# Attention scan and two expert layers in one program: all transfers on SyncE's and ScalarE's queues, a chunk's period of 25 steps, and ScalarE alone reading the stages' sums

## The chip, the cores and the metric

The kernel runs on one core of a Trainium2 chip. The metric is the device time of one execution in microseconds (us), and the figure for a kernel is the median over its runs. The core has five instruction streams that run side by side and meet only at semaphores: TensorE (PE in the profile, with its weight loads as PEld), VectorE (DVE), ScalarE (ACT), GpSimd (POOL) and SyncE (SP). A transfer is issued by an instruction in one of these streams and then carried out by the core's 16 DMA engines. Each stream works strictly in order, so an instruction that waits holds up all that stands behind it in its stream.

## What is computed

Three layers follow each other on 3072 tokens (4 sequences of 768) of 384 features. First comes a linear attention with a complex decay, whose state is 48 x 48 for each of 8 heads:

```python
for t in range(S):
    ar, ai = (a_re_n[:, :, t, :, None], a_im_n[:, :, t, :, None])
    new_re = ar * S_re - ai * S_im
    new_im = ar * S_im + ai * S_re
    kv = np.einsum('bhd,bhe->bhde', k[:, :, t], v[:, :, t])
    S_re, S_im = (new_re + kv, new_im)
    y[:, :, t] = np.einsum('bhd,bhde->bhe', q[:, :, t], S_re)
```

Then four experts, `out += p[:, e] * (relu(x @ w1[e]) @ w2[e])`, each with 1024 hidden features, and at last `max(0.01 * h, h) @ w_out` with `h = x @ w_in` and 2048 hidden features. The weights of the last layer arrive as 64-bit numbers.

## The kernel before

**The dense layers are the frame.** The tokens are worked in 6 groups of 512. A hidden block of 128 features is a *unit*: units 0 to 31 are the four experts (the first stage of a group), units 32 to 47 the last layer (the second stage). `order` (lines 357 to 365) lists all units of all groups: the first stages of groups 0, 1 and 2, then the second stage of group 0, and from there a first stage and the second stage of two groups earlier in turn, with the last two second stages at the end. The first 8 units of group 0 are run in two halves of 256 tokens. To keep accuracy, each operand is split into a high and a low part, so a unit costs 18 matmuls of 512 columns: 9 in `gemm_in` (L421) into `ph`, from which VectorE and ScalarE make `hp` and its parts `hh` and `hl` (L426 to L439), and 9 in `gemm_out` (L450 to L452), which add to the three sums `acc`. `gemm_in` runs two units ahead of `gemm_out`.

**Weights.** The experts' weights are loaded once (`raw`, L380), split by ScalarE and GpSimd (L396, L397), stored split in `ws_scratch` (L400), and loaded from there whenever the unit comes up again (L388), five units ahead, into 7 buffers. The last layer's weights are decoded from 64-bit numbers in the background (`decode`), loaded at L324 and stored at L351.

**Ends of stages.** At the end of a first stage the three sums become the input of the second: ScalarE copies each to `x2h` (L591) and VectorE subtracts it from the sum to give `x2l` (L592). At the end of a second stage ScalarE copies each sum to `o`, which has two buffers, and issues its transfer to the output (L601, L602). The next stage's first product into a sum waits until the sum has been read.

**The attention runs in between.** A chunk is 128 tokens; there are 24, four to a group. `elementwise(c)` makes the decayed features `ft` from the inputs `aaqk` on VectorE, ScalarE and GpSimd, and its last step sends `ft` in six transfers into `hd` (L247), which has the heads' features on the partitions. `products(c)` transposes `ft` (`pt`, L261), multiplies the features in `hd` to scores `sc` (L274), and goes on to `y`. Both are generators; `background()` calls one step at a time. Chunks 0 to 3 follow the written-out order `PLAN`. From chunk 4 on, a period of 23 calls and one empty one holds the 8 steps of `products(c)` at the calls in `PSTEPS` and the steps of `elementwise(c + 1)` at the others. `pace` spreads the calls evenly over the units, up to 3 behind each half of a unit, so that a group's four chunks are ready when its first stage begins. The program fixes the order within each stream; nothing is reordered at run time.

**Which queue issues what, before.** SyncE: the inputs, the raw and split weights, `hd` of chunks 0 to 3. GpSimd: `hd` from chunk 4 on and two of chunk 1, the stores of the split weights, and all of the decoder's transfers. ScalarE: the output.

## Time and profile before

| what | value |
|---|---|
| median of 3 runs | 1519.18 us (1519.04 to 1524.72) |
| the profiled execution | 1522.4 us, of which 1520.7 us are the span from its first to its last instruction |
| TensorE busy | 1414.4 us, 93% of the span |
| VectorE busy | 875.1 us, 58% |
| ScalarE busy | 557.1 us, 37% |
| GpSimd busy | 350.2 us, 23% |
| read and written in HBM | 262.72 MB and 42.52 MB |
| granted TensorE clock, mean over the span | 0.971 of full speed |

The busy shares are means over stages with different limits: the first 85 us are filled by the start of the attention, up to 640 us the attention of the next groups runs beside first stages, up to 1130 us beside first and second stages in turn, and behind that dense units stand alone. Sums of waits say who waited for whom, but a wait costs time only where the waiting engine sets the end. TensorE's clock has two levels, 1.2 and 2.4 GHz; the profile gives the granted clock of a stretch as a mean share of the higher one.

### The profile page before, as it was taken

Reading aid. Unit: us, or ns where it says so; the run is one execution under the profiler, and the core shown is the slowest. Engines: PE = TensorE matmul, PEld = TensorE weight load, DVE = VectorE, ACT = ScalarE, POOL = GpSimd, SP = SyncE. Lnnn points to the kernel's source line nnn. Section 1 sums busy time; section 2 is a strip of 40 time slices with the busy share of each in tenths; the row PEclk is TensorE's granted clock in tenths of the full one; section 3 lists DMA queues with packets and bytes.
Section 4 is the critical chain, followed back from the end, with each engine's and each line's share of the span. In section 5 each row is a group of like instructions: output and inputs, shape, how many; then the busy total and the mean of one; then the engine's idle time right before and its main releaser. Section 6 shows DMA issues by size and latency. Waiting matters only on the chain.

```text
span 1520.7 us, 18523 instructions
## 1 busy us (share of the span) xinstructions
PE 1414.4 (93%) x6972; PEld 1183.8 (78%) x6972; DVE 875.1 (58%) x1521; ACT 557.1 (37%) x939; POOL 350.2 (23%) x451
## 2 busy tenths in 40 slices
PE   1898998998998999899999999999999999999996
PEld 0797877786877887687888887888887888887875
DVE  8848777668888787875554554554533333332331
ACT  4535554434334333354233344233332111332232
POOL 5134677334333333321111111111100000000000
PEclk9789999999999999999999999999999999999998
DMA  6398778787778979768568568567556665555551
GB/s 245 50 290 283 247 250 261 220 271 214 241 271 249 285 262 289 208 217 244 180 209 238 170 197 244 180 203 208 157 183 205 210 196 196 195 187 180 187 195 44
DMA packets 75235, 325.49 MB, mean 214 GB/s; under 512 B 10464, under 2 KB 16448, under 8 KB 75136
## 3 DMA queue, kind: packets, MB, share of 16 engines
q1 hardware_dynamic: 56960, 253.10, 53.2%
q0 software_dynamic: 15584, 66.40, 14.8%
q10 hardware_dynamic: 2592, 4.72, 0.9%
q8 instruction: 56, 0.92, 0.3%
q14 instruction: 43, 0.35, 0.1%
HBM read 262.72 MB, written 42.52 MB: 201 GB/s over the span
## 4 chain that ended last, share of the span: by engine, by line
PE 62%; DVE 16%; DMA 6%; ACT 5%; issue 5%; POOL 4%; SPq 0%; ACTq 0%; DVEq 0%; POOLq 0%
PE ph L421 27%; PE acc L450 9%; PE acc L452 9%; PE acc L451 9%; DMA hd<-ft 4%; DVE hl L439 3%; PE sc L274 2%; PE py L297 2%; PE py L299 2%; DMA out_dram<-o 2%; ACT hh L438 2%; DVE hp L426 1%; DVE ft L238 1%; PE pm L285 1%; POOL hd L247 1%
## 5 line engine op out<-in xcount | busy, mean ns | idle before, releaser
L421 PE MATMUL ph<-xh,wt 128*128 128x512 f32 (+1 forms) x1200 | 400.7, 390 | 1.9 <-ACT wt L396 0.9
L450 PE MATMUL acc<-hh,wt 128*128 128x512 f32 (+1 forms) x888 | 357.2, 402 | 23.1 <-DVE x2l L592 11.0
L452 PE MATMUL acc<-hl,wt 128*128 128x512 f32 (+1 forms) x888 | 346.6, 390 | 3.3 <-DVE hl L439 3.0
L451 PE MATMUL acc<-hh,wt 128*128 128x512 f32 (+1 forms) x888 | 345.3, 389 | 0.0
L438 ACT CAST hh<-hp 128x512 fp32r<-128x512 f32 (+1 forms) x296 | 180.3, 609 | 416.7 <-DVE hp L426 345.0
L439 DVE TENSOR_TENSOR hl<-hp,hh 128x512 fp32r<-128x512 f32 (+1 forms) x296 | 218.3, 737 | 195.4 <-ACT hh L438 194.5
L421 PEld LDWEIGHTS ph<-xh,wt 128*128 128x128 f32 x1200 | 228.4, 193 | 45.8 <-ACT wt L396 1.1
L421 PE MATMUL ph<-xl,wt 128*128 128x512 f32 (+1 forms) x600 | 231.9, 386 | 0.0
L426 DVE SCALAR_TENSOR_TENSOR hp<-ph,pb 128x512 f32<-128x512 f32 (+1 forms) x200 | 133.1, 665 | 171.0 <-PE ph L421 170.5
L450 PEld LDWEIGHTS acc<-hh,wt 128*128 128x128 f32 x888 | 170.2, 192 | 57.7 <-ACT o L601 12.1
L452 PEld LDWEIGHTS acc<-hl,wt 128*128 128x128 f32 x888 | 169.6, 191 | 41.9 <-DVE hl L439 7.5
L421 PE MATMUL ph<-x2h,wt 128*128 128x512 f32 x576 | 199.0, 400 | 0.0
L451 PEld LDWEIGHTS acc<-hh,wt 128*128 128x128 f32 x888 | 170.6, 192 | 30.3
L429 DVE SCALAR_TENSOR_TENSOR hp<-hp 128x512 f32<-128x512 f32 x96 | 68.6, 715 | 180.9 <-ACT hp L428 180.9
L421 PEld LDWEIGHTS ph<-xl,wt 128*128 128x128 f32 x600 | 115.9, 193 | 21.0 <-DVE xl L316 0.3
L421 PEld LDWEIGHTS ph<-x2h,wt 128*128 128x128 f32 x576 | 109.4, 190 | 25.3
L428 ACT COPY hp<-ph 128x512 f32<-128x512 f32 x96 | 56.2, 585 | 176.3 <-PE ph L421 175.5
L421 PE MATMUL ph<-x2l,wt 128*128 128x512 f32 x288 | 115.0, 399 | 0.0
L247 POOL DMA_DIRECT2D hd<-ft x122 | 64.9, 540 | 151.0 <-DVE ft L238 112.5
L274 PE MATMUL sc<-hd 96*128 96x128 f32 x384 | 57.8, 300 | 24.7 <-DMA hd<-ft 20.9
L274 PEld LDWEIGHTS sc<-hd 96*128 96x128 f32 x384 | 55.3, 212 | 30.8 <-issue 13.2
L397 POOL TENSOR_TENSOR wt<-raw,wt 128x384 fp32r<-128x384 f32 x64 | 68.9, 1094 | 41.8 <-ACT wt L396 41.4
(98 smaller groups left out, 1525.2 us busy)
## 6 DMA issues: line engine op xcount, KB each, us to landing
wt<-ws_scratch SPq DMA_DIRECT2D x264, 768.0 KB, 4.6
ws_scratch<-wt POOLq DMA_DIRECT2D x32, 768.0 KB, 7.2
aaqk<-in_attn_dram SPq DMA_DIRECT2D x22, 768.0 KB, 8.6
hd<-ft POOLq DMA_DIRECT2D x122, 128.5 KB, 9.4
raw<-in_w_dram SPq DMA_DIRECT2D x32, 384.0 KB, 6.7
r<-in_w_dram POOLq DMA_DIRECT2D x32, 384.0 KB, 5.1
ws_scratch<-dw POOLq DMA_DIRECT2D x32, 384.0 KB, 5.6
pb<-pn_scratch SPq DMA_DIRECT2D x24, 256.0 KB, 5.0
```

The source lines that it names most:

```text
L247: (G if c >= CPG or c in HDG and i == ri else SP).dma_start(hd[row : row + DG], ft[:, ri, i])
L274: PE.matmul(sc[:, j], hd[:, h, P : 2 * P], hd[:, h, :P], start=True, stop=True)
L397: G.tensor_tensor(wt[:, 1], raw, wt[:, 0].bitcast(F32), ALU.subtract)
L421: PE.matmul(ph[:, : t1 - t0], wt[:, wi, cols], x[kc][:, t0:t1], start=n == 0, stop=n == 3 * NG - 1)
L426: V.scalar_tensor_tensor(hp, ph, 0.0, pbs[g, u // 8][:, t0:t1], ALU.max, ALU.mult)
L428: A.copy(hp, ph)
L429: V.scalar_tensor_tensor(hp, hp, 0.01, hp, ALU.mult, ALU.max)
L438: A.copy(hh, hp)
L439: V.tensor_tensor(hl, hp, hh.bitcast(F32), ALU.subtract)
L450: PE.matmul(out, wt[:, 0, cols], hh, start=first, stop=False)
L451: PE.matmul(out, wt[:, 1, cols], hh, start=False, stop=False)
L452: PE.matmul(out, wt[:, 0, cols], hl, start=False, stop=last)
```

## The change

All transfers that GpSimd issued go to SyncE (two of chunk 1 to ScalarE). The transfers into `hd` move from the end of `elementwise(c)` into a step of their own, `by_head`, at call 1 of the next period for chunks from 4 on. The store of a unit's split weights moves from the end of its splitting to the unit's own place in the order, in front of `gemm_out`. In the decoder the next load comes one call later, and a store is issued one block later. A period has 16 elementwise steps and 9 steps of products, 25 calls and an empty one: the phase's scan, its reduction to one turn and its limits are three steps, and the two halves of `ft` are two. `vt` has its buffers beside those of `aaqk`. At the end of a stage ScalarE copies the three sums, one behind the other, to `o`, which has three buffers; at a first stage's end `x2h` is a copy of `o` and `x2l` is made from both by GpSimd.

```diff
...
 DEC = 33.0
-PSTEPS = (3, 7, 8, 11, 13, 15, 18, 22)
-NSTEPS = 23
+PSTEPS = (1, 3, 5, 8, 10, 13, 16, 18, 21)
+ESTEPS = 16
+NSTEPS = ESTEPS + len(PSTEPS)
 WAIT = 4
...
                 t = pool.tile([P, 4, NG, P], F32, name="aaqk", bufs=2)
-                vt = p_in.tile([P, DM], F32, name="vt", bufs=4)
+                vt = pool.tile([P, DM], F32, name="vt", bufs=2 if c in (1, 3) else 3)
                 inputs[c] = (t, vt)
...
                 V.tensor_tensor_scan(th[:, i], ones, r[:, i], first, ALU.mult, ALU.add)
+            if c >= CPG:
+                yield
             V.tensor_scalar(g, th, 1.0 / TWO_PI, MAGIC, ALU.mult, ALU.add)
...
             T.tensor_tensor(th, th, g, ALU.subtract)
+            if c >= CPG:
+                yield
             V.tensor_scalar(th, th, -PI, PI, ALU.max, ALU.min)
...
                 )
-            yield
+                if i or c >= CPG:
+                    yield
+            feats[c] = (ft, vt)
+            if c < CPG:
+                by_head(c)
+        def by_head(c):
+            ft, vt = feats[c]
+            pool = p_el2 if c in (1, 3) else p_el
             hd = pool.tile([2 * D, H, 2 * P + 1], F32, name="hd")
...
                     row = ri * D + i * DG
-                    (G if c >= CPG or c in HDG and i == ri else SP).dma_start(hd[row : row + DG], ft[:, ri, i])
+                    (A if c in HDG and i == ri else SP).dma_start(hd[row : row + DG], ft[:, ri, i])
             feats[c] = (ft, hd, vt)
...
         def products(c):
+            if c >= CPG:
+                by_head(c)
+                yield
             ft, hd, vt = feats.pop(c)
...
                 raw64[i] = pools["dec"].tile([P, DM, 2], I32, name="r64", bufs=3)
-                G.dma_start(
+                SP.dma_start(
                     raw64[i].rearrange("p a b -> p (a b)"),
...
                 )
+        stored = []
...
             G.tensor_tensor(wt[:, 1], wo, wt[:, 0].bitcast(F32), ALU.subtract)
+            yield
             load_raw64(i + 3)
-            yield
-            G.dma_start(ws[NU1 + u][:, half], wt.bitcast(F32))
+            if stored:
+                SP.dma_start(*stored.pop())
+            stored.append((ws[NU1 + u][:, half], wt.bitcast(F32)))
...
                 del raws[s]
-                G.dma_start(ws[order[s][1]], wts[s].bitcast(F32))
...
                     yield from decode(i)
+                yield
+                SP.dma_start(*stored.pop())
...
             for g in range(1, NGRP):
-                pace.append((begins[g] - MARGIN, first + 14 + (NSTEPS + 1) * CPG * g))
+                pace.append((begins[g] - MARGIN, first + ESTEPS + (NSTEPS + 1) * CPG * g))
             pace.append((1e9, pace[-1][1] + 1))
...
                 return u in (NU1, NU1 + 1) and order[s - 1 - (u - NU1)][:2] == (g, NU1 - 1)
+            def evacuate(acc):
+                out = [pools["x2"].tile([P, TG], F32, name="o", bufs=NG) for _ in acc]
+                for o, a in zip(out, acc):
+                    A.copy(o, a)
+                return out
...
                 split_h(s + 2, hp)
+                if fresh[s]:
+                    SP.dma_start(ws[u], wts[s].bitcast(F32))
                 gemm_out(s, acc)
...
                 if u == NU1 - 1:
+                    evacuated = evacuate(acc)
                     x2[g] = ([], [])
-                    for dc in range(NG):
+                    for dc, o in enumerate(evacuated):
                         xh = pools["x2"].tile([P, TG], F32R, name=f"x2h{dc}", bufs=LAG + 1)
                         xl = pools["x2"].tile([P, TG], F32R, name=f"x2l{dc}", bufs=LAG + 1)
-                        A.copy(xh, acc[dc])
-                        V.tensor_tensor(xl, acc[dc], xh.bitcast(F32), ALU.subtract)
+                        A.copy(xh, o)
+                        G.tensor_tensor(xl, o, xh.bitcast(F32), ALU.subtract)
                         x2[g][0].append(xh)
...
                 elif u == NU - 1:
-                    for dc in range(NG):
-                        o = pools["x2"].tile([P, TG], F32, name="o", bufs=2)
-                        A.copy(o, acc[dc])
+                    for dc, o in enumerate(evacuate(acc)):
                         A.dma_start(outT[dc * P : (dc + 1) * P, g * TG : (g + 1) * TG], o)
...
```

## Rows read from the trace of the kernel before

**Rows 1.** Busy us by engine (instructions), granted clock, DMA share, GB/s; a late stretch

```profile
1300.00:1340.00 40.00, 40.00 (x175) 32.68 (x175) 15.34 (x23) 13.53 (x23) 0.00 (x0) 1.00 0.57 193
```

**Rows 2.** TensorE's waits from 100 to 440 us: total us, times, longest

```profile
PE sc L274 <- DMA hd<-ft: 19.2, 5, 5.8
```

**Rows 3.** TensorE's waits in the whole span, same columns

```profile
PE acc L450 <- DVE x2l L592: 11.0, 2, 6.4
PE acc L450 <- ACT o L601: 10.0, 5, 3.2
```

**Rows 4.** The view of rows 1 for stretches around waits of TensorE

```profile
139.00:154.00 15.00, 12.41 (x64) 10.81 (x63) 11.04 (x16) 6.18 (x11) 8.37 (x10) 0.77 0.95 329
...
288.00:303.00 15.00, 11.25 (x62) 9.72 (x61) 8.03 (x17) 5.01 (x7) 1.86 (x2) 0.89 0.70 222
374.00:390.00 16.00, 10.16 (x44) 8.70 (x44) 12.38 (x23) 7.90 (x14) 6.12 (x8) 0.79 0.88 293
468.00:485.00 17.00, 12.39 (x57) 10.41 (x56) 14.12 (x27) 6.68 (x13) 3.61 (x6) 0.90 0.79 285
633.00:650.00 17.00, 10.58 (x40) 8.33 (x39) 10.92 (x19) 8.64 (x16) 6.51 (x11) 0.80 0.99 225
...
1371.00:1384.00 13.00, 9.84 (x31) 7.54 (x30) 2.77 (x4) 3.00 (x5) 0.00 (x0) 0.74 0.50 168
```

**Rows 5.** Line 790, the program's end: count, ns min/median/max, first and last start

```profile
L790 POOLq DRAIN  x3: 50/107/9215, 1510.6 to 1520.4; - x3
L790 SPq DRAIN  x3: 7/7/7, 1512.9 to 1520.1; - x3
```

**Rows 6.** Timeline, a second stage's end: start, us, instruction, idle before and releaser

```profile
1369.57 0.59 ACT L601 COPY o<-acc 128x512 f32<-128x512 f32 x1 [0.46 <-ACT o L601]
...
1374.59 0.59 ACT L601 COPY o<-acc 128x512 f32<-128x512 f32 x1 [4.43 <-DMA out_dram<-o]
...
1375.22 0.80 PE L450 MATMUL acc<-hh,wt 128*128 128x512 f32 x1 [3.16 <-ACT o L601]
```

**Rows 7.** Timeline, a first stage's end (629 to 643 us)

```profile
630.91 1.82 DVE L238 TENSOR_TENSOR ft<-cs,aaqk 128x768 f32<-128x768 f32 x2
...
638.64 1.55 ACT L591 CAST x2h<-acc 128x512 fp32r<-128x512 f32 x3
...
639.38 1.88 DVE L592 TENSOR_TENSOR x2l<-acc,x2h 128x512 fp32r<-128x512 f32 x3
...
640.12 0.80 PE L450 MATMUL acc<-hh,wt 128*128 128x512 f32 x1 [6.42 <-DVE x2l L592]
```

**Rows 8.** Timeline, chunk 8 from its features to its scores (270 to 293 us)

```profile
271.97 1.82 DVE L238 TENSOR_TENSOR ft<-cs,aaqk 128x768 f32<-128x768 f32 x2
...
274.38 3.31 POOL L247 DMA_DIRECT2D hd<-ft  x6 [1.89 <-DVE hl L439]
...
292.51 0.77 PE L274 MATMUL sc<-hd 96*128 96x128 f32 x2 [3.75 <-DMA hd<-ft]
```

**Rows 9.** Issues of hd (columns: rows 11) from 0:100, 360:426, 1030:1110 us

```profile
hd<-ft SPq DMA_DIRECT2D x22, 128.5 KB, 5.6
...
hd<-ft POOLq DMA_DIRECT2D x12, 128.5 KB, 12.0
...
hd<-ft POOLq DMA_DIRECT2D x12, 128.5 KB, 6.7
```

**Rows 10.** Line 247, columns as in rows 5

```profile
L247 POOL DMA_DIRECT2D hd<-ft x122: 530/532/714, 42.0 to 1097.3; - x122
...
L247 SPq DMA_DIRECT2D hd<-ft x22: 547/601/688, 37.0 to 81.0; - x22
```

**Rows 11.** DMA issues of the whole span: count, KB each, median us to landing

```profile
wt<-ws_scratch SPq DMA_DIRECT2D x264, 768.0 KB, 4.6
ws_scratch<-wt POOLq DMA_DIRECT2D x32, 768.0 KB, 7.2
```

**Rows 12.** SyncE's waits in the whole span: total us, times, longest

```profile
SPq L147 <- DVE ft L238: 30.4, 10, 6.0
```


## The prediction

> **What bounds the kernel now.** The span is bounded by TensorE (PE), so the views were read in this order: what TensorE waited for, what its clock was after each wait, and then the place of each wait. In an undisturbed late stretch TensorE issues 175 matmuls of 512 columns in 40 us [rows 1], which is 0.229 us each, or 4.11 us for a unit of 18. Nothing in the change makes that stream shorter, so a gain can come only from time in which TensorE stands still or runs slowly. The list of waits has three entries that the change touches: the scores (`sc`) wait for the transfer into `hd`, 19.2 us in 5 waits between 100 and 440 us [rows 2]; the first product of a new stage waits for `x2l` (11.0 us in 2) and for `o` (10.0 us in 5) [rows 3]. Behind such a wait the granted clock falls to the lower level, 1.2 GHz, for some us: the stretch from 139 us has a mean granted share of 0.77, so 15 x 0.23 = 3.45 us of full speed are missing [rows 4]. Four stretches around the waits for `hd` are like this (0.77 three times, 0.79 once over 16 us) and one of 15 us has 0.89: 3 x 3.45 + 3.36 + 1.65 = 15.4 us. The two waits for `x2l` cost 17 x 0.10 + 17 x 0.20 = 5.1 us in this way, and of those for `o` only the one at 1375 us, 13 x 0.26 = 3.4 us [rows 4]. The last view is the end of the program: GpSimd's (POOL's) drain takes 9.2 us from 1510.6, while SyncE (SP) is at its own drain, 0.007 us long, at 1512.9 [rows 5].
>
> **The change part by part.** The sum is made against the profiled execution, 1522.4 us with a span of 1520.7; the median of the runs is 1519.18, 0.2% less, and the differences carry over.
>
> **1, the end of the program: -6.9 us.** Ahead of the long drain GpSimd has issued all its transfers, the 122 of `hd` [rows 10] and those of the split weights and of the decoder, and it has no other drain between them and that one. After the change GpSimd issues none. If the length comes from them, the end is set by SyncE at 1512.9 instead of 1510.6 + 9.2 = 1519.8: 6.9 us. If the drain is as long without transfers, nothing. I take 6.9, because GpSimd's two drains behind it, with no transfer since the drain before, take 0.05 and 0.11 us [rows 5].
>
> **2, the ends of the second stages: -13.4 us.** With two buffers for `o` the third copy waits until the first transfer out has landed: the second copy begins at 1369.57, the third at 1374.59 after 4.43 us of waiting, and TensorE stood 3.16 us [rows 6]. With three buffers, all copied before the first transfer is issued, the third copy would end near 1370.8, before the product that needs the sum. All of the 10.0 us goes, and the 3.4 us of clock with it. Bounds: 10.0 and 13.4, and the row for the higher one is the stage end that is shown.
>
> **3, the ends of the first stages: -5 us.** Here ScalarE copies the three sums out and `x2l` is made from the copy by GpSimd. The sum is then free when the copy ends and not when VectorE's subtraction ends. But ScalarE itself came late: its first copy began at 638.64 and TensorE went on at 640.12, when the first subtraction had ended [rows 7], so with a copy of 0.59 us [rows 6] this saves only 640.12 - (638.64 + 0.59) = 0.9 us, 1.8 for both. VectorE was late because of what stood in its queue, of which 1.82 us were `ft` at 630.91 [rows 7]; with 25 steps this chunk's `ft` comes just behind the stage's end, another 1.8. Of the 5.1 us of clock I count 1.5. Together 5; the bounds are 0 and 16.1. The three more copies of ScalarE (1.55 / 3 = 0.52 us each [rows 7]) and GpSimd's subtractions lie beside TensorE: `x2` is read 32 units, or 131 us, later at the soonest; without that cover they would cost 1.6 us and more at each of six ends.
>
> **4, the transfer into `hd`: +5 us.** This is the term in doubt. Chunk 8 shows the path: `ft` ends at 273.79, GpSimd issues six transfers, and the scores begin at 292.51 after 3.75 us of waiting [rows 8]. So TensorE came 15.0 us after `ft`, and the transfer needed 18.7. Both numbers change. The time that it has shrinks: before, `ft` is made in call 19 of a chunk's 24 and the scores in call 8 of the next, 13 calls later; after, `ft`'s second half is in call 24 of 26, so 10 calls. For chunks 8 to 11, 96 calls were spread over 32 units and 104 are now: 13 / 3.0 = 4.33 units against 10 / 3.25 = 3.08, or 1.25 units x 4.11 = 5.1 us less, which leaves 9.9. What it needs shrinks as well. The lower bound is SyncE's six issues (5 x 0.60 us) and its median of 5.6 us to landing in the first 100 us, 8.6 us [rows 9, 10]; the upper is chunk 8's own 18.7. In between lies the order of the queue: SyncE issues the next chunk's input right ahead of `hd`, and a load of that size (768 KB) lands in 4.6 us [rows 11]: 8.6 + 4.6 = 13.2. That is the value I take, as it is made of rows for the same queue. Chunk 8 then waits 13.2 - 9.9 = 3.3 us, about as now. Chunks 4 to 7 have more calls to a unit and less time, so I let the 19.2 us grow by 5 and keep the clock's 15.4. If the waits went, the term would be -(19.2 + 15.4) = -34.6; with 18.7 us at all eight chunks it is 8 x (8.8 + 3.4) - 34.6 = +63. From chunk 12 on there are 13 / 2 = 6.5 units before and 10 / 2.17 = 4.6 after, 18.9 us, more than any of these needs.
>
> **5, what queues up behind on SyncE: +3 us.** Weight loads, `hd`, the next input, the split weights' stores and the decoder's transfers now share one queue. At a chunk's boundary a weight load may stand behind SyncE's wait for `ft` (the longest so far 6.0 us) and six issues of 0.6 us, 9.6 us in all [rows 10, 12]. A load is issued when a buffer is freed and needed four units, 16.4 us, later, and lands in 4.6 us [rows 11]; 2.2 us are left. So it is nearly always hidden; if the landing takes longer, it shows as a wait of the unit's first product for `wt`. The stores of the split weights come three units later. The first eight units go through in halves of 2.1 us, and a unit's second load is issued three halves, 6.2 us and some attention work, behind its store, which took 7.2 us to land from GpSimd's queue [rows 11]; here a few us may show once. Bounds 0 and 10, taken 3. What GpSimd no longer issues costs nothing and gives nothing on the path: no wait of TensorE names it. The tile `vt` keeps a buffer for each chunk that is in use, and ScalarE's two transfers for chunk 1 take the place of GpSimd's two: nothing for either.
>
> The sum: -6.9 - 13.4 - 5 + 5 + 3 = -17.3, so 1505.1 for the profiled execution and 1519.2 - 17.3 = **1502 us** for the median.
>
> **Rivals.** *A, the scores wait longer.* `ft` comes three calls closer to its readers and the transfer gains less from SyncE's queue than I count. For it speaks that the load on the DMA engines seems to set the landing: GpSimd's own transfers take 12.0 us in a loaded stretch and 6.7 in a light one [rows 9]. At 16 us from `ft` to landing each of eight chunks waits 6.1 us and loses 3.4 of clock: 8 x 9.5 - 34.6 = +41 in the place of +5, which gives 1538. It makes the kernel slower than before by more than can be measured from 14.6 us on (8 x (4.7 + 3.4) - 34.6 = +30). The Trainium skill, DMA: Bandwidth & Descriptors, section Issuing engines are not separate DMA queues, states that all issuing engines feed the same 16 DMA engines and that another issuer saves only the time of issuing; by that rule `hd` lands no sooner and this rival holds, and the trace agrees as far as the two medians for GpSimd go. *B, the waits for `hd` go.* The elementwise steps are spread over more calls, so VectorE may reach `ft` with less delay, and `hd` stands in order on one queue in the place of sharing the engines with weights: 1502 - 5 - 34.6 = 1462. Against it: three calls fewer. The Trainium skill, SBUF — State Buffer, section SBUF: two separate sides, states that transfers issued by GpSimd wait for descriptors while VectorE holds a shared port, and run at full speed when issued from SyncE or ScalarE; by that rule B holds, but here GpSimd's issues take 0.53 us each with 0.71 the longest [rows 10], so the delay lies behind the issue. *C, two parts don't do what they say.* The drain is long without transfers too, and ScalarE's copies come as late as VectorE's subtractions did: 1502 + 6.9 + 5 = 1514.
>
> **Chances.** Forecast 0.52 (its own range 1490 to 1513), A 0.19, B 0.14, C 0.15. About 0.5%, 7.6 us, is what a measurement of this kernel can tell from no change, so "same" is 1511.6 to 1526.8. Faster: 0.46 of the forecast's 0.52, B, and a third of C, 0.65. Same: 0.06 + 0.02 of A + 0.10 of C, 0.18. Slower: 0.17, all A. For 8 in 10 the range leaves out the far parts of A and B: 1470 to 1533.
>
> **What would show it.** Step 1: GpSimd's drain at the end well under 1 us and the span's end near 1513 plus what precedes it. Step 2: no wait of `acc` for `o`. Step 3: waits of `acc` at the first stages' ends shorter by about 1 to 2 us each, now put down to `o`. Step 4: the waits of `sc` for `hd` at 20 to 30 us in all with the same number of falls of the clock; 60 and more would be A, under 5 B. Step 5: a wait of `ph` for a weight transfer of a few us in all. The prediction is wrong if the order of SyncE's queue costs more than one issue behind another, as would show in long waits of SP on `ft` with TensorE waiting for weights.

## The result and the profile after

The changed kernel takes 1506.78 us (median of 6 runs, 1500.60 to 1511.02) against 1519.47 us (median of 6): 0.9906 of the time before, 95% interval 0.988 to 0.9933. It is faster by 0.9%, as forecast; the time lies 4.8 us above the 1502 us and inside the range. The profiled execution took 1506.07 us with a span of 1504.2 us, 16.5 us less than the span before. The traces below are of one execution each, and that pair lies further apart than the medians do (12.7 us).

TensorE's waits over the whole span of the changed kernel (total us, times, longest) answer to [rows 2, 3]:

```profile
...
PE sc L292 <- DMA hd<-ft: 26.7, 7, 7.1
...
PE acc L471 <- ACT o L586: 6.9, 2, 4.2
PE sc L292 <- ACT hh L459: 6.3, 1, 6.3
PE ph L442 <- DMA wt<-ws_scratch: 6.3, 5, 2.2
...
PE sc L292 <- ACT tb L119: 1.5, 1, 1.5
...
```

The five waits for `o` at the ends of second stages are gone. Two waits at the ends of first stages are left, now put to `o`. A new one is that for weights (`wt`). And the scores wait longer: the rows that name `hh` and `tb` are chunks 10 and 8, whose last transfer into `hd` landed 0.1 to 0.4 us before the scores began, so they count as waits for `hd` too. Without 0.9 us at chunk 1 that makes 26.7 - 0.9 + 6.3 + 1.5 = 33.6 us.

The granted clock in the stretches around these waits (columns as in [rows 1]), the changed kernel:

```profile
139.00:154.00 15.00, 14.06 (x78) 12.25 (x78) 10.12 (x20) 6.94 (x13) 6.45 (x7) 0.89 0.48 146
181.00:196.00 15.00, 14.82 (x75) 13.00 (x76) 7.64 (x15) 4.97 (x8) 3.01 (x3) 0.83 0.39 155
...
385.00:400.00 15.00, 15.00 (x72) 12.85 (x73) 11.95 (x24) 5.02 (x8) 2.01 (x2) 0.81 0.83 321
...
475.00:492.00 17.00, 14.90 (x79) 12.66 (x79) 11.84 (x21) 8.40 (x16) 6.54 (x5) 1.00 0.87 323
...
641.00:656.00 15.00, 13.51 (x53) 10.89 (x54) 11.02 (x17) 7.10 (x14) 4.22 (x3) 0.89 0.47 141
1364.00:1378.00 14.00, 14.00 (x63) 11.43 (x62) 4.66 (x7) 5.67 (x10) 0.00 (x0) 1.00 0.76 261
```

The seven stretches behind waits for `hd` (139, 181, 222, 261, 385, 431 and 541 us; three are shown) lack 14.6 us of full speed, against 15.4 before. Behind the second stages' ends nothing is missing any more, behind the first stages' 15 x 0.11 = 1.7 us against 5.1.

How a second stage now ends (timeline, 1366 to 1369 us, answering to [rows 6]):

```profile
1366.31 1.07 ACT L586 COPY o<-acc 128x512 f32<-128x512 f32 x2
...
1366.92 0.34 ACTq L633 DMA_DIRECT2D out_dram<-o  x1
1367.26 0.60 ACT L586 COPY o<-acc 128x512 f32<-128x512 f32 x1
1367.41 0.90 ACTq L633 DMA_DIRECT2D out_dram<-o  x2
...
1368.33 0.39 PE L471 MATMUL acc<-hh,wt 128*128 128x512 f32 x1
```

All three sums are out at 1367.86, before TensorE needs the first of them.

And the program's end (columns as in [rows 5], with ScalarE's last issues behind it):

```profile
L821 POOLq DRAIN  x3: 34/45/82, 1496.3 to 1504.0; - x3
L821 SPq DRAIN  x3: 7/7/7, 1503.1 to 1503.4; - x3
```

```profile
1494.96 1.34 ACTq L633 DMA_DIRECT2D out_dram<-o  x3
```

GpSimd's drain is down from 9.2 us to under 0.1, and SyncE sets the end. But SyncE comes to its drain 8.3 us after TensorE's last product started (1494.8), where it was 6.2 us before. The three outputs are issued together, and each lands 1.6 to 1.7 us behind the one ahead (at 1497.0, 1498.6 and 1500.3): the last one 5.5 us behind that product, where it was 5.1. The larger part stands behind it: from the last landing to its drain SyncE takes 2.8 us, where it took 1.1.

Both kernels run the same 296 units in the same order, so the starts of a unit's first product can be set side by side. "Step" is what the difference grew by since the row above:

| up to | before, us | after, us | difference | step |
|---|---|---|---|---|
| unit 16, start of the attention | 133.4 | 131.2 | -2.2 | -2.2 |
| unit 70, scores of chunks 4 to 11 | 448.9 | 455.1 | +6.3 | +8.5 |
| unit 77, end of a first stage | 486.5 | 489.3 | +2.8 | -3.5 |
| unit 106, chunks 12 to 14 | 631.1 | 636.0 | +4.9 | +2.1 |
| unit 108, end of a first stage | 648.3 | 650.4 | +2.2 | -2.7 |
| unit 284, all ends of second stages but the last | 1452.8 | 1440.9 | -11.9 | -14.1 |
| end of the span | 1520.7 | 1504.2 | -16.5 | -4.6 |

### The profile page after: what moved, and what is told of

Read it like the earlier page. It is cut to its first block, busy times and chain, and to the rows that moved or that the text cites. A ratio compares the mean times of both kernels' runs of the same rounds, so it can differ in the third digit from the quotient of the medians.

```text
span 1504.2 us, 18506 instructions
## 1 busy us (share of the span) xinstructions
PE 1403.8 (93%) x6972; PEld 1177.8 (78%) x6972; DVE 864.8 (57%) x1503; ACT 566.7 (38%) x957; POOL 263.6 (18%) x251
## 4 chain that ended last, share of the span: by engine, by line
PE 60%; DVE 8%; DMA 3%; ACT 2%; issue 2%; POOL 0%; SPq 0%; DVEq 0%; ACTq 0%; POOLq 0%
PE ph L442 27%; PE acc L471 9%; PE acc L473 9%; PE acc L472 9%; DVE hl L460 2%; PE sc L292 1%; PE py L315 1%; PE py L317 1%; DMA vt<-in_v_dram 1%; DVE hp L447 1%; ACT hh L459 1%; DMA ws_scratch<-dw 1%; PE pm L303 1%; DVE ft L243 1%; DMA r<-in_w_dram 1%
## 5 line engine op out<-in xcount | busy, mean ns | idle before, releaser
L442 PE MATMUL ph<-xh,wt 128*128 128x512 f32 (+1 forms) x1200 | 407.5, 396 | 6.9 <-DMA wt<-ws_scratch 6.3
L471 PE MATMUL acc<-hh,wt 128*128 128x512 f32 (+1 forms) x888 | 350.0, 394 | 6.9 <-ACT o L586 6.9
L473 PE MATMUL acc<-hl,wt 128*128 128x512 f32 (+1 forms) x888 | 341.9, 385 | 0.0
L472 PE MATMUL acc<-hh,wt 128*128 128x512 f32 (+1 forms) x888 | 341.2, 384 | 0.0
L460 DVE TENSOR_TENSOR hl<-hp,hh 128x512 fp32r<-128x512 f32 (+1 forms) x296 | 213.5, 721 | 183.6 <-ACT hh L459 183.1
L447 DVE SCALAR_TENSOR_TENSOR hp<-ph,pb 128x512 f32<-128x512 f32 (+1 forms) x200 | 133.4, 667 | 199.9 <-PE ph L442 199.8
L471 PEld LDWEIGHTS acc<-hh,wt 128*128 128x128 f32 x888 | 167.5, 189 | 38.2 <-ACT o L586 7.6
L472 PEld LDWEIGHTS acc<-hh,wt 128*128 128x128 f32 x888 | 167.7, 189 | 31.0
L450 DVE SCALAR_TENSOR_TENSOR hp<-hp 128x512 f32<-128x512 f32 x96 | 72.3, 753 | 171.7 <-ACT hp L449 171.7
L442 PEld LDWEIGHTS ph<-x2h,wt 128*128 128x128 f32 x576 | 108.7, 189 | 25.2
L292 PE MATMUL sc<-hd 96*128 96x128 f32 x384 | 58.3, 302 | 35.8 <-DMA hd<-ft 26.7
L208 POOL TENSOR_TENSOR aaqk<-aaqk,ge 128x384 f32<-128x384 f32 x24 | 26.5, 1103 | 252.1 <-DVE ge L207 252.1
```

The source lines that it names most:

```text
L208: G.tensor_tensor(q, q, en, ALU.mult)
L292: PE.matmul(sc[:, j], hd[:, h, P : 2 * P], hd[:, h, :P], start=True, stop=True)
L442: PE.matmul(ph[:, : t1 - t0], wt[:, wi, cols], x[kc][:, t0:t1], start=n == 0, stop=n == 3 * NG - 1)
L447: V.scalar_tensor_tensor(hp, ph, 0.0, pbs[g, u // 8][:, t0:t1], ALU.max, ALU.mult)
L450: V.scalar_tensor_tensor(hp, hp, 0.01, hp, ALU.mult, ALU.max)
L460: V.tensor_tensor(hl, hp, hh.bitcast(F32), ALU.subtract)
```

## The experiments

All ratios are to runs of the kernel before on the same chip, with a 95% interval. For chunks 8 to 11 two times are read from each trace: what the transfer into `hd` needed, from the end of `ft` to its last landing, and what it had, from the end of `ft` to the time when TensorE would have begun the scores without waiting for it.

| kernel | `hd` needed, us | `hd` had, us | median, us | ratio |
|---|---|---|---|---|
| before | 18.6, 15.3, 18.6, 17.3 | 15.0, 18.7, 13.0, 16.4 | 1519.5 | 1 |
| after | 12.8, 11.9, 13.8, 12.3 | 11.4, 12.0, 7.9, 9.8 | 1506.8 | 0.9906 |
| hd_pool | 15.8, 16.8, 16.5, 16.0 | 11.4, 12.0, 9.8, 9.8 | 1541.7 | 1.0146 (1.0121 to 1.0172) |
| hd_first | 8.7, 9.3, 8.6, 8.6 | 11.3, 11.8, 7.4, 8.8 | 1486.8 | 0.9788 (0.9766 to 0.9809) |
| late_scores | 11.0, 10.9, 10.7, 12.1 | 13.2, 15.8, 13.8, 15.4 | 1486.6 | 0.9764 (0.9738 to 0.9790) |
| hd_first_late | 8.7, 9.1, 8.7, 8.7 | 13.2, 15.8, 13.8, 13.7 | 1472.6 | 0.9681 (0.9655 to 0.9707) |
| period_back | 8.7, 8.7, 8.7, 8.7 | 15.2, 18.7, 16.8, 16.8 | 1483.9 | 0.9751 (0.9727 to 0.9776) |

**The ends of the stages alone, and undone.** ends_alone is the kernel before with this part of the diff and the place of `vt`, which makes room for the third `o`:

```diff
-                        A.copy(xh, acc[dc])
-                        V.tensor_tensor(xl, acc[dc], xh.bitcast(F32), ALU.subtract)
+                        A.copy(xh, o)
+                        G.tensor_tensor(xl, o, xh.bitcast(F32), ALU.subtract)
...
-                        o = pools["x2"].tile([P, TG], F32, name="o", bufs=2)
```

> The kernel before with the new ends of stages alone: ScalarE copies the three sums one behind the other into three buffers, x2l is made by GpSimd from the copies (vt moves beside aaqk, as in the change, to make room); queues and period as before. Theory: steps 2 and 3 of the prediction stand by themselves: -13.4 and -5, so 18 us less than before, 1501; no wait of acc for o at the second stages' ends, two waits of 2 to 5 us at the first stages' ends. The drain of GpSimd stays 9.2 us but begins sooner, as the last outputs are issued sooner, which may give another 2 us. Rival: the time is given back at the scores, which stay bound by their transfer: under 9 us less, 1510 or more.

Measured 1505.28 us, ratio 0.991 (0.9889 to 0.9931), between the two expectations. Its span is 17.2 us shorter: 18.9 us before TensorE's last product, of which some 14 at the second stages' ends and 5 at the first, and 1.7 us given back at the end, where GpSimd still drains for 9.2 us but begins only when the last of the three outputs has landed. The 2 us that were to come on top did not come. ends_back is the changed kernel with these lines turned round again.

> The changed kernel with the old ends of stages (VectorE subtracts from the sum, two buffers for o with a transfer behind each copy); queues and period as changed. Theory: the same 18 us come back, 1525, with five waits of acc for o of 10 us in all and two for x2l of 11 us; the queues and the period by themselves then lose about 5 us against before, although the program's end gains 4 to 7. Rival: with the new order of VectorE the old ends cost less than 9 us, 1515 or less.

Measured 1517.99 us, ratio 0.9987 (0.9974 to 1.0001): 11 us come back, between the two expectations. The waits for `o` at second stages return; those at the first stages, in ends_back and in ends_alone, are

```profile
PE acc L471 <- DVE x2l L617: 8.5, 2, 4.5
```

```profile
PE acc L450 <- ACT o L563: 7.7, 2, 5.6
```

In the changed kernel the new ends take this waiting from 8.5 us to 6.9, in the kernel before from 11.0 to 7.7. So at a first stage's end the copies themselves save 1.6 to 3.3 us of waiting for both ends together. By the unit starts of the table above, the clock included, they save more: at these two places they make the kernel before 4.6 us shorter (ends_alone), and the changed kernel is 3.5 us shorter there than ends_back. The other 2.6 us come off in ends_back too, with the old ends; that VectorE's changed order does this is argued.

**The order on SyncE's queue.** hd_first issues the next but one input behind `hd` and not ahead of it; nothing else moves.

```diff
-                    if c + 2 < NCHUNK:
-                        load_chunk(c + 2)
...
                         next(todo if k in PSTEPS else ahead, None)
+                        if k == PSTEPS[0] and c + 2 < NCHUNK:
+                            load_chunk(c + 2)
```

> The changed kernel with one step of the order moved: the next but one chunk's input (aaqk and vt) is issued behind the six transfers into hd in SyncE's queue, and no longer ahead of them. Theory: the input ahead of them costs its two issues (1.2 us) and about its own landing (4.6 us by the weight loads of that size), so ft to the last landing falls from 11 to 14 us to 7 to 9 us, the waits of sc from 34 us to under 8 us, most falls of the clock with them: 1465 to 1480. Rival: the landing is set by the load on the 16 engines and not by the order in the queue: hd lands only the 1.2 us of issuing sooner, 1495 to 1500, and the falls of the clock stay.

Measured 1486.83 us, 20 us less than the changed kernel, between the two ranges. Chunk 10 in the changed kernel and in hd_first (timelines):

```profile
369.85 0.94 DVE L243 TENSOR_TENSOR ft<-cs,aaqk 128x768 f32<-128x768 f32 x1
370.83 0.33 SPq L148 DMA_DIRECT2D aaqk<-in_attn_dram  x1
...
371.68 3.87 SPq L261 DMA_DIRECT2D hd<-ft  x6
...
384.97 1.40 PE L292 MATMUL sc<-hd 96*128 96x128 f32 x5 [6.31 <-ACT hh L459]
```

```profile
355.34 0.95 DVE L243 TENSOR_TENSOR ft<-cs,aaqk 128x768 f32<-128x768 f32 x1
356.31 3.78 SPq L261 DMA_DIRECT2D hd<-ft  x6
360.14 0.59 SPq L148 DMA_DIRECT2D aaqk<-in_attn_dram  x1
...
365.37 0.82 PE L292 MATMUL sc<-hd 96*128 96x128 f32 x5 [1.65 <-ACT kt L280]
```

Around chunks 10 and 11 a transfer into `hd` lands a median of 8.3 us after its issue in the changed kernel and 4.5 us in hd_first. `hd` now needs 8.6 to 9.3 us, the lower bound of the prediction's step 4. It was too little for "under 8 us of waits", as chunks 5 to 7 still have only 5.7 to 7.2 us; the waits for `hd` put down by name fall to 11.8 us.

**Another issuer for `hd`.** In hd_pool GpSimd issues the six transfers of chunks from 4 on, at the same place; in hd_act ScalarE does (A for G in this line):

```diff
-                    (A if c in HDG and i == ri else SP).dma_start(hd[row : row + DG], ft[:, ri, i])
+                    (A if c in HDG and i == ri else G if c >= CPG else SP).dma_start(hd[row : row + DG], ft[:, ri, i])
```

> The changed kernel with the transfers into hd of chunks from 4 on issued by GpSimd, at the same place in the order; all else on SyncE and ScalarE. Two questions. First the queue: if GpSimd's queue itself is slow (15 to 18 us from ft to landing before), the scores wait 3 us longer at each of eight chunks, about 1530 to 1540; if what counts is standing behind the input in SyncE's queue, hd lands sooner than now, 1480 to 1495. Second the end: GpSimd then issues 120 transfers and not 218. If its drain goes by their number it takes 5.1 us and is hidden beside SyncE's own end, if it is a fixed price of having issued any it takes 9.2 us and the end comes 2 to 3 us later than SyncE's.

Measured 1541.72 us, 35 us slower than the changed kernel and just above the range for a slow queue. At chunk 10 GpSimd begins to issue 0.6 us behind `ft` and is done in 3.3 us, neither later nor slower than SyncE, but the last landing comes 2.6 us later, although nothing stands ahead of `hd` in GpSimd's own queue:

```profile
386.10 0.33 SPq L148 DMA_DIRECT2D aaqk<-in_attn_dram  x1
...
386.63 3.27 POOL L261 DMA_DIRECT2D hd<-ft  x6 [2.85 <-DVE d L360]
...
386.99 0.38 SPq L410 DMA_DIRECT2D wt<-ws_scratch  x1
...
390.01 0.49 SPq L372 DMA_DIRECT2D ws_scratch<-dw  x1
...
390.60 1.19 SPq L410 DMA_DIRECT2D wt<-ws_scratch  x2
...
402.72 1.19 PE L292 MATMUL sc<-hd 96*128 96x128 f32 x4 [6.85 <-DMA hd<-ft]
```

So from GpSimd's queue the transfer takes 3 to 4 us longer (means of the table: 16.3 us against 12.7). That the queue itself is slower isn't shown by this, as SyncE's queue runs on beside it: within 5 us of GpSimd's first issue SyncE issues five more transfers, among them three weight loads. In the changed kernel, where `hd` stands ahead of them, none of them is issued until 6.8 us behind the first of the six (378.50). The Trainium skill, DMA: Bandwidth & Descriptors, section Issuing engines are not separate DMA queues, holds that another issuer saves only the time of issuing; hd_pool doesn't contradict it, as the traffic beside `hd` isn't the same. The Trainium skill, SBUF — State Buffer, section SBUF: two separate sides, says that transfers issued by GpSimd can be held up and those of SyncE and ScalarE are not. The direction agrees, but in the next run ScalarE's first three are as late, and no run here shows the cause it names.

> The changed kernel with the transfers into hd of chunks from 4 on issued by ScalarE, at the same place in the order; the next but one input still goes ahead on SyncE. Theory (it is standing behind the input in one queue that costs the 4 us): on ScalarE's queue hd has nothing in front of it, so ft to the last landing is 9 to 10 us as in the kernel with hd first, and apart from ScalarE's six issues (3.6 us of ScalarE at each chunk) the time is near 1487: 1485 to 1495. Rival (all queues share the 16 engines, so another issuer gains only the 1.2 us of issuing): hd lands as late as in the changed kernel, 11 to 13 us, and ScalarE's issues delay hh: 1505 to 1515.

Measured 1618.56 us, ratio 1.064 (1.0605 to 1.0675), outside both. ScalarE took up to 14 us for six issues:

```profile
296.06 14.17 ACTq L261 DMA_DIRECT2D hd<-ft  x6
```

The fourth is issued at 302.92, when the first has landed (302.90), the fifth at 307.36 behind a weight load of SyncE's (landed at 307.34), the sixth at 309.68 behind a store of SyncE's (309.66); `hh` and the sums' copies wait behind them in ScalarE's stream. The trace names the semaphores that tell of the landings: as these programs were built, the transfers of SyncE and ScalarE share eight, an issue waits until the transfer that last used its semaphore has landed, and in no trace are more than eight of the two engines' transfers under way. GpSimd's have eight of their own. So the change also halved the places: 77 of the 630 issues in the changed kernel begin within 0.12 us of the landing of the eighth transfer ahead of them, 6 of 412 before. In the changed kernel weight loads wait in SyncE's queue for the landings of `hd` and of the input (SyncE's waits):

```profile
SPq L410 <- DMA hd<-ft: 14.7, 28, 1.5
...
SPq L410 <- DMA aaqk<-in_attn_dram: 8.3, 7, 2.9
```

ScalarE's first three transfers of a chunk have none ahead of them in their own queue, and they are no sooner for it: at chunks 8 to 11 they land 7.8, 8.7 and 10.0 us after their issue (means), in hd_pool 6.8, 9.9 and 10.9, in the changed kernel 7.5, 7.8 and 8.0, and in hd_first 3.3, 4.0 and 4.5. So a queue of its own does not spare `hd` what is under way beside it, which speaks for the rival, that all queues share the engines. It isn't the input alone, as weight loads and stores of SyncE's run beside `hd` here as well. What hd_first shows is that issuing the input later takes 4 us off; that the order within the queue does it is not shown.

**The time that `hd` has.** late_scores moves the steps of products behind the transfers three calls later, the last one two; hd_first_late joins it with hd_first.

```diff
-PSTEPS = (1, 3, 5, 8, 10, 13, 16, 18, 21)
+PSTEPS = (1, 6, 8, 11, 13, 16, 19, 21, 23)
```

> The changed kernel with all steps of products behind the transfers into hd three calls later in the period (6, 8, 11, 13, 16, 19, 21, 23 in the place of 3, 5, 8, 10, 13, 16, 18, 21). Theory (the wait is the need minus the time between): three calls are 3/3.25 units, 3.8 us, for chunks 8 to 11 and about 3 us before, so the 34 us of waits at nine chunks fall to some 10 us and about half of the falls of the clock go: 1480 to 1492. Rival: the steps of the next chunk's features, which move forward to fill the calls, end as late as before and the products now come later for the group that needs them, so waits of ph for xl at the group's start take the place: 1505 or more.

Measured 1486.61 us: 20 us less than the changed kernel, as the theory has it, from 2 to 6 us more time for `hd` (which also needs 1.5 us less, 11.2 on average).

> Both edits together: hd ahead of the next but one input in SyncE's queue, and the products three calls later. Theory: hd needs 8.6 to 12 us and gets about 3 us more than in the kernel with the first edit alone, so its 13 us of waits for hd go with the falls of the clock behind them (4 times 3.4 us): 1460 to 1475. Rival: what is left there is bound by VectorE's lateness (ft itself), so that scores three calls later only move the wait: 1482 to 1487.

Measured 1472.64 us, ratio 0.9681 (0.9655 to 0.9707): the fastest kernel of the study, 34 us below the changed one and 47 below the one before. Its four largest waits between 100 and 660 us:

```profile
PE px L325 <- ACT y L321: 7.5, 4, 2.9
PE sc L292 <- DMA hd<-ft: 6.0, 2, 3.2
PE ph L442 <- DMA wt<-ws_scratch: 3.8, 5, 1.2
PE acc L471 <- ACT o L586: 3.3, 2, 3.0
...
```

**The old period with the new queues.** period_back takes PSTEPS, the 23 steps, whole features and by_head at the end of elementwise back; queues and ends stay changed (the diff is cut).

```diff
-PSTEPS = (1, 3, 5, 8, 10, 13, 16, 18, 21)
-ESTEPS = 16
-NSTEPS = ESTEPS + len(PSTEPS)
+PSTEPS = (3, 7, 8, 11, 13, 15, 18, 22)
+NSTEPS = 23
...
-                if i or c >= CPG:
-                    yield
+            yield
             feats[c] = (ft, vt)
-            if c < CPG:
-                by_head(c)
+            by_head(c)
...
```

> The changed kernel with the old period: 23 steps, whole features in one step, and the six transfers into hd issued by SyncE at the end of elementwise, 13 calls ahead of the scores and ahead of the next input in the queue; queues and ends of stages as changed. Theory (distance and order in the queue set the waits): the scores come 4.1 units, 17 us, behind ft at chunks 8 to 11, hd needs 8.6 to 10 us as in the kernel with hd ahead of the input, so no wait of sc is left from chunk 8 on and at most 8 us in all before it: 1470 to 1485. Rival: the 23-step period itself was the cost, as its steps hold more of VectorE's work each and hh and hl come late: waits of acc and of ph for VectorE and ScalarE take the place, 1500 or more.

Measured 1483.88 us, inside the theory's range. Together with ends_alone this splits the change: the ends take 1519.5 to 1505.3, the queues take that to 1483.9 (-21), and the new period takes it to 1506.8 (+23; by the ratios -24 and +24). With the period goes the place of by_head, which now stands behind the next but one input; hd_first takes 20 of these 23 us off by that order alone, late_scores as much by the calls between. The scores hardly wait here, but the weights do, because SyncE stands at the transfers into `hd` until VectorE has made `ft` (first fence: SyncE's waits; second: TensorE's, 100 to 660 us):

```profile
SPq L254 <- DVE ft L238: 158.2, 20, 21.8
```

```profile
PE ph L432 <- DMA wt<-ws_scratch: 16.1, 7, 3.9
```

That is the first mechanism of the prediction's step 5, seen in full: at 499 us, the longest of the seven, the load is issued at 492.85, behind the six of `hd`, for which SyncE stood from 481.6 to 487.65 until `ft` was made. In the changed kernel `hd` and the input ahead of it are issued in the next period, when `ft` is mostly made: SyncE waits for `ft` 35.6 us at the one, 21.1 of them in the first chunk, and 64.3 us at the other.

**The decoder's and the weights' transfers back on GpSimd.** dec_pool and store_pool put these two kinds, each by itself, back on GpSimd (of the decoder's, the loads as well):

```diff
-                SP.dma_start(*stored.pop())
+                G.dma_start(*stored.pop())
```

```diff
-                    SP.dma_start(ws[u], wts[s].bitcast(F32))
+                    G.dma_start(ws[u], wts[s].bitcast(F32))
```

> The changed kernel with the decoder's 64 transfers (32 loads, 32 stores) issued by GpSimd at their places, all else on SyncE and ScalarE. Two questions. The end: 120 transfers into hd from GpSimd left a drain of 1.2 us, 218 of all kinds one of 9.2. If the drain goes by the kind (rows or bytes in a transfer), the decoder's leave several us; if by how recent the last one is or by the number, 0.7 us or less. The queue: SyncE waits 161 us for the decoder's buffers in the changed kernel; if this delays weight loads, the waits of ph for wt (6.3 us in 5) go and the time falls by 5 to 10 us, 1497 to 1502; if it is hidden, 1505 to 1510.

> The changed kernel with the 32 stores of the split weights issued by GpSimd at their new place; all else on SyncE and ScalarE. The drain at the end: 120 transfers into hd left 1.2 us, 64 of the decoder 5.3 us, all 218 together 9.2 us. If it adds up by kind, 32 stores leave 9.2 - 1.2 - 5.3 = 2.7 us; if it goes by how late in the program the last one was issued, under 0.5 us, as these end in the first third. The time: no wait but those of ph for weights in the first 130 us should change, 1503 to 1510.

Measured 1513.90 us (0.9957, 0.9939 to 0.9976), 4 us above the higher of its two ranges, and 1510.31 us (0.994, 0.9917 to 0.9963), at the upper end of its own; neither gains. Taking the decoder off SyncE's queue leaves the waits for weights as they were, 6.0 us in 5, so its 161 us of waiting in that queue delayed no weight that mattered. GpSimd's drain at the end, in hd_pool, dec_pool and store_pool:

```profile
L821 POOLq DRAIN  x3: 44/107/1217, 1538.1 to 1539.9; - x3
```

```profile
L821 POOLq DRAIN  x3: 44/107/5292, 1505.2 to 1511.5; - x3
```

```profile
L821 POOLq DRAIN  x3: 44/107/2679, 1499.5 to 1502.8; - x3
```

The three kinds add up: 1.2 + 5.3 + 2.7 = 9.2 us, the drain of before. So the drain does come from GpSimd's transfers, and not by their number alone: 120 into `hd` leave 10 ns each, 64 of the decoder and 32 stores 83 and 84 ns each.

**What is left in the fastest kernel.** spread gives `y` to `px` four calls in the place of two; spread_hold also holds the decoder for one unit ahead of a first stage's end.

```diff
-PSTEPS = (1, 6, 8, 11, 13, 16, 19, 21, 23)
+PSTEPS = (1, 6, 8, 11, 13, 16, 18, 20, 24)
...
-                    if now > DEC:
+                    if now > DEC and u != NU1 - 2:
```

> The kernel with hd ahead of the input and late products, with its last three steps moved: py's second half at 18, y at 20 and px at 24 (19, 21, 23 before). Theory: px waits 17.1 us in 9 for ScalarE's copy of y there, as only two calls lie between; with four calls this falls to under 5 us, so the time falls by about 10 us, to 1458 to 1466. Rival: ScalarE's copy comes as much later as the call does, or the wait moves to the first unit of a group, which needs px's result one call later: 1470 to 1475.

> The same with the decoder held for one unit ahead of each first stage's end. In the changed kernel the copies of the sums to o stood in ScalarE's queue behind hh, which waited for hp, which stood on VectorE behind the decoder's steps (2.4 us of them at 640 us, 1.3 us at 475 us). Theory: that row of work is what step 3 of the prediction left over; without the decoder's steps the waits of acc for o at the two stage ends fall from 3 to 7 us in all to under 3 and the time by 3 to 6 us against the kernel without the hold. Rival: hh comes as late for ScalarE's own work (tables and attention) and nothing is gained, within 2 us.

Measured 1473.88 us (0.97, 0.9672 to 0.9729) and 1474.33 us (0.9703, 0.9675 to 0.9731): neither differs from hd_first_late. The theory's 17.1 us in 9 were the waits of TensorE and of its weight loads together; TensorE itself waited 7.5 us in 4, so there was less to gain. In spread `px` waits no more, but the steps that came nearer to each other do:

```profile
...
PE acc L471 <- ACT o L586: 5.3, 2, 4.2
...
PE pm L303 <- DVE att L293: 3.4, 3, 2.5
PE py L315 <- DVE att L293: 2.5, 1, 2.5
...
```

In spread_hold the waits for `o` fall to 2.8 us, without a gain that the runs can tell. What stood ahead of the copies is seen in the changed kernel's timeline at 640 us, answering to [rows 7]:

```profile
638.54 0.56 DVE L366 SCALAR_TENSOR_TENSOR d<-d,d 128x384 f32<-128x384 f32 x1
639.17 0.51 ACT L367 CAST dw<-d 128x384 fp32r<-128x384 f32 x1 [3.20 <-issue]
639.59 0.58 ACT L449 COPY hp<-ph 128x512 f32<-128x512 f32 x1
...
640.20 1.10 DVE L450 SCALAR_TENSOR_TENSOR hp<-hp 128x512 f32<-128x512 f32 x1 [1.11 <-ACT hp L449]
641.34 0.62 ACT L459 CAST hh<-hp 128x512 fp32r<-128x512 f32 x1 [1.17 <-DVE hp L450]
641.86 1.56 ACT L586 COPY o<-acc 128x512 f32<-128x512 f32 x3
...
642.49 0.50 PE L471 MATMUL acc<-hh,wt 128*128 128x512 f32 x1 [4.22 <-ACT o L586]
```

ScalarE stands at the decoder's `dw` until VectorE has made `d`, and copies `ph` only behind it: 1.7 us after `ph`'s last product started (637.88), where it takes 0.5 us in the dense part (at 1488.8). So the decoder's steps hold up `hp` by some 1.2 us, that `hh`, and that the copies, which stand behind `hh` in ScalarE's stream. The rest of the 4.22 us is that row of work itself.

## Why the prediction was right, step by step

**Step 1, the end (-6.9): -4.6.** The cause holds: without GpSimd's transfers there is no long drain, and the three kinds add up to the 9.2 us. The step counted SyncE's drain as fixed, and behind TensorE's last product it comes 2.1 us later. Of this 0.4 us are the later landing of the last output. From that landing to its drain SyncE takes 2.8 us; it took 1.1 before, 1.4 in ends_alone with the outputs issued together, and 2.4 in ends_back with the outputs as before but all transfers on SyncE. So most of it came with the transfers that SyncE took over.

**Step 2, the second stages' ends (-13.4): -14.1**, with all five waits gone and the clock at 1.00 behind all five; ends_alone has -14.2 in the same rows.

**Step 3, the first stages' ends (-5): -6.2.** The working holds in outline: the copies come late on ScalarE, and by themselves save 1.6 us of waiting in the changed kernel (1.8 was taken), with the clock 3.5 us (ends_back). The wait is now put to `o`. What stands ahead of them at 640 us are the decoder's steps and the row from `hp` to `hh`; the prediction had named VectorE's `ft`.

**Step 4, the scores (+5): about +13.** Both numbers of the working were near: `hd` needed 12.7 us (mean of chunks 8 to 11) where 13.2 was taken, and had 10.3 where 9.9 was taken. The split of the 13.2 into 8.6 and the input's 4.6 holds in size: with the input behind, 8.6 to 9.3. That it is the order within the queue is not shown; hd_act and hd_pool speak for the shared engines. What was mis-sized is chunks 4 to 7, put in with a share of the 5 us: they had only 6.7 to 9.2 us and waited 21.4 us, where they had waited 9.6. So the waits for `hd` of chunks 4 to 11 grew from 20.4 us to 32.1. And from chunk 12 on, where the step gave the transfer 18.9 us, it had 12.5 to 17.4, and chunk 13 waited another 1.7 us. The clock lost nearly the same as before (14.6 us against 15.4), as taken.

**Step 5, SyncE's queue (+3): 6.3 us of waits for `wt`**, inside the bounds of 0 and 10. Three of the five, 3.2 us, come at 121 to 129 us, in the units that go through in halves: their loads took 5.0 to 9.2 us to land, where 4.6 was counted, and the step had named a longer landing as the way it would show. The other two, 3.1 us at 540 and 600 us, are of loads that were held until one of the eight transfers ahead had landed (issued at 532.68, behind a landing at 532.62); this the prediction did not have. The wait for `ft`, which it named first, shows in period_back, among 16.1 us of waits for `wt`.

**What made the sum come out.** Steps 4 and 5 gave some 19 us and not 8; yet the table has only -2.2 + 8.5 + 2.1 = +8.4 us for that part of the program. The row of 8.5 closes: TensorE's waits grew from 23.3 us to 32.1 in it, and what the lower clock cost outside the waits fell by 0.3. The rest was not in the prediction: before, TensorE also waited for other work between 126 and 590 us, 3.0 us for `hl`, 1.8 for `hh`, 1.3 for weights still being split and 2.5 for `y`, of which 0.3 us for `y` is left. The 25 steps are not the reason for `hl` and `hh`: period_back, with 23, has no such waits either, while ends_alone, with the old queues, has 7.4 us of them, so that comes with the queues. For `y` it may be the steps, as period_back still waits 2.3 us. Another 2.9 us, between units 77 and 106, are neither in the waits that the trace lists nor in the clock and stay open, and the start's -2.2 us lies within what other kernels with that start show (-0.5 in period_back, -3.5 in hd_first). So the forecast was right by its mechanisms, and as near as it was by luck: two errors of some 11 us went against each other.

**The rivals.** A has its mechanism but not its price: the transfer needed 12.7 us, below the 14.6 from which it was to decide; on GpSimd's queue, with 16 us, it does decide, and hd_pool's 1541.7 is near the 1538 worked out for it. B, the waits going altogether, is nearly what the queues do by themselves (-21 us; in period_back 3.6 us of waits of the scores are left); the change took it back by the shorter time between `ft` and the scores and by the input ahead of `hd`. C fell: the drain is short.

## What to carry to other kernels

Where a transfer is waited for, read two numbers from the trace, what it needs and what it has, and move either: here some 4 us less of the one or 4 us more of the other gave 20 us each, most of it by several chunks that waited and by the clock behind each wait. A part of a change that gains by itself (the queues) can be hidden by one that costs as much (the new period and the place of `hd` in it); undo them one by one. Before an issue is put on a shared queue, ask what that queue waits for: a transfer whose data are not yet made holds up all that stands behind it, and so does a landing when eight transfers are under way already.

## What the hardware showed that was not expected

GpSimd's drain at the program's end has a price by the kind of transfer it has issued: 83 ns for each of the decoder's and 84 ns for each store of split weights, 10 ns for each transfer into `hd`, and the three add up. What sets the price is open: bytes don't (the decoder's and the stores are 25.2 MB each and left 5.3 and 2.7 us). Three outputs issued within 1.3 us landed 2.1, 3.2 and 4.4 us after their issue.

Waits of like length can lower the clock or leave it. Chunk 4's wait of 2.6 us in the kernel before stands in a stretch with a granted share of 0.77 [rows 4]; waits of 2.8 and 3.2 us at chunks 5 and 6 in hd_first_late (columns as in [rows 1]) leave it at 1.00, and what decides isn't shown:

```profile
174.00:190.00 16.00, 15.31 (x92) 13.60 (x93) 12.39 (x23) 8.04 (x14) 7.68 (x8) 1.00 0.87 326
209.00:225.00 16.00, 15.82 (x96) 13.88 (x97) 10.37 (x20) 7.37 (x13) 7.82 (x7) 1.00 0.78 309
```
